# Residue-first keys and values for the strided heads, a new order of their value products, and a new plan

## The chip, the cores and the metric

The kernel runs on one core of one Trainium2 chip. The metric is the device time of one execution in microseconds (us); lower is better. A run gives the median of several executions, and one more execution is recorded by the hardware profiler.

## The reference

Inputs are q, k and v of shape 8 x 8 x 576 x 64 (batch, head, position, head width) and the weights of a mixture of four experts. First comes attention with two masks: heads 0 to 3 see the last 32 positions ("local"), heads 4 to 7 see every earlier position with the same position modulo 32 ("strided"):

```python
scores = scale * np.matmul(q, k.transpose(0, 1, 3, 2))
rel = pos[:, None] - pos[None, :]
mask_local = (rel >= 0) & (rel < 32)
mask_strided = (rel >= 0) & (pos[None, :] % 32 == pos[:, None] % 32)
attn = softmax(np.where(mask, scores, -1e9))     # mask by head
x = np.matmul(attn, v)                           # heads side by side: 8 x 576 x 512
```

Then, for each of the four experts, causal attention of width 64 over x (products with wq, wk, wv, all scores, softmax, product with wo); a gate picks two experts for each position and weights their outputs. The output is 8 x 576 x 512, float32.

## The kernel before, in words

**Stages.** Work is done by batch (8) and head pair (`hp`, 4 per batch: two local, two strided). `stage1(b, hp)` does the masked attention of one head pair; its result, transposed, goes as a high and a low part (`xh`, `xl`) into `project` (products with wq and wk), `values2` (product with wv, gate), `attend` (the experts' attention) and `out_tile` (product with wo, store).

**Strided stage 1.** There are 16 such stages (8 batches, 2 head pairs). Since position p sees only positions of its residue p mod 32, the work is cut by residue: 18 positions share one residue, and three residues at a time form a block of 54 queries against 54 keys, 11 blocks in all (the last has two residues). The steps:

- `load` (L454) brings q and k as 32 x 32 pieces into `nat`, eight DMAs of 32 partitions per head pair. `turn` (L465) transposes each of the two in one VectorE instruction (128 x 576) into `qkt`, where head width lies on partitions and positions along the row. For q the output is written residue first (a strided write, so that the 18 positions of a residue are neighbours); for k it is written in the order of positions.
- `scores` (L509) multiplies 64 x 64 quarters of TensorE's array: stationary is a run of 64 queries, moving are 54 keys. As k is in the order of positions, the moving operand is a pattern of 18 groups of 3 neighbours, 32 positions apart. A product of float32 is two instructions, so 24 products are 48 matmul records for each stage. The four quarters (row half by head, column half by block) are taken in turn.
- `mask`, `softmax` on VectorE, GpSimd and ScalarE; `tps2` (L568) transposes the probabilities; two copies bring them to `ptt`.
- `load_v` (L483) brings V by residue: 6 parts of 2 DMAs. Each DMA has the 18 positions of one residue of each of 5 or 6 blocks, and writes them to 18 partitions, every third one: within a block the key order is position first, residue second (`vt.t[64 * hb + r:64 * hb + r + 52:3, ...]`).
- `values1` (L619) multiplies V (stationary, 54 x 64) with the transposed probabilities (moving, 54 columns): 22 products, 44 matmul records. The row half of the array is the block's parity `hb`, the column half is the head `h`. The loops run over `i` (head and block, the head outermost), `hf`, `hb`: for one head's 11 products two quarters take turns, and then the other two.

**The order of the work.** Nothing in the program's loops sets the order: every operation is put down as an `Op` with an engine, and `PLAN`, a list of 2555 words, gives the order in which they are issued and, in the digits at a word's end, the buffer that each new tile takes (`223P564044` is operation 223 on TensorE with six new buffers). Some copies may stand on ScalarE or VectorE (letters A and D). Each engine works through its part of the list in that order; so does SyncE, from whose queue all DMAs are issued (634 of them). Buffers: `nat` 3, `qkt` 2, `v1` 3, PSUM banks 8.

Of the kernel before, what the change touches and what calls it, by code (L numbers as in the profile page):

```python
# [20 lines left out]
def attention_moe_kernel(  # L21
# [12 lines left out]
    nc = tc.nc  # L34
    B, H, S, D = q.shape
# [4 lines left out]
    STR = 32  # L40
    NJ = S // STR
# [49 lines left out]
    def op(kind, eng, n, key, fn, r=(), w=(), mode=None, npk=0, after=()):  # L91
# [24 lines left out]
        82S0 0P0 84S 4S1 40S2 41S 3S 39S 1S 42S 81S 52S0 2S 172S0 78S 80S 50S 5P120 160S1 8P34 6D 7A 43P561 11S1 10A  # L116
        46P70 9D 45A 44D 119S1 15P210 47A 48A 173A0 13S 174D0 53P431 117S 17D 161A0 16D 118S 162G0 19D0 121S 54D 21G
        55D 123S 23A 56D1 57D 77S 58G 18D 79S 59G 25D 60A 62D 122S 20G 61A 63D 129S2 22A 64D 83S 24D 66G 26D 12S 65G
        85D0 14S 27G 124S 28G 67D0 157S 120S 86D 169S 29D1 93P650 175S2 51S 126D1 30P701200 158A 163S3 95D 159G 49S
        94D 170A 91S1 97D2 37A 171G 33A 96D 35A 88S 31A 38D 176A 36D 98G 34D 87S 125D 164A 99G 100A 90S 68P435611  # L120
        177G 101A 92S 102D 165G 103D 133P211 89S 71A 32D 69A 104D 73A 75A 132S 70D 106G 1157P00 74D 134D 130S 1151P7
        105G 135D 1191P41 136D3 131S 1197P5 72D 138G 76D 107P211 184S0 137D 1192P 140A 139G 109D 108A 128S 142D 141A
        110P3622 205S2 143D 1163P1 187S1 113A 144D 115A 114D 1158P 111A 145G 116D 185A0 1169P2 178S 112D 146G 186D0
        1159P 127S 1164P 166S 147P630 202S 1170P 149A 148D 181S 188A 1193P 1198P 179A 189D 150P3633 180D 190S 1152P
        167A 271S0 155A 168D 1165P 153A 151A 156D 203S 1153P 154D 152D 1171P 182A 211S0 1199P 183D 1172P 199S 191A
        1160P 192D 1173A 204S 1166P 1161A 1174D0 1154P 234S1 1167A 1162D 1175G0 1178P60 1155A 1168D 235S 1156D 209S
        1221P320 200S 1179A 1216P010 1222D0 1247P760 245S1 1218D 1224A 1223D 201S 1226P310 1217D 1220A 1249D1 1219A
        1194P 210S 1225A 1228D 1176P2 206S 1195A 1227D 1230A 1248D 267S 1229A 1196D1 1182P0 237S 1177A 207D0 1251A
        232S 1231D 1250A 233S 1200P 208D 1184P6 212S 1183A 1201A 265S 1202D 302S2 213P131 1185A 236S 240D1 1203P7
        239S 215D 1180P4 238S 214D 216D1 276S2 1254P20 280S 1181A 217G 1204P 1186D00000 272S 1209P0 1205P 266S 218A  # L130
        269S 241D 1187A 301S 1188D 246P560 268S 242S 219D 1232G 1210P 193S0 1190G 1236G 247D 304S 1211P 248D 1233G
        220D 303S 1212P 1234G 273D0 1252P3 270S 1213A 221G 1238P141 1189S 1240A 307S 1214D 1239A 1237G 1253D 243S
        194A0 222D1 1215G1 244S 1255D 223P564044 279S 274D 195G0 1256A 338S1 249D0 1206P 341S 228A 1235G 224A
        281P130 229D 230A 226A 225D 314S0 1207A 250G 231D 1257D 300S 1208D 283D 1275P241 1258G 277S 251A 282D
        1241P500 1276D2 369S0 1280P731 1259G 284D2 1278A 1261P122 1242A 306S 1260G 1281D 1262A 1282D 1243A 312S
        1285P571 1277D 1283A 285G 252D 1264P133 337S 1284A 1267P04 1287D 372S 1279A 286A 1286D 1311P71 311S 253D
        1289A 1244P500 287D 305S 254G 1288A 1312D3 278S 1268A 288D 1265A 335S 1290D 289G 1245A 255D0 1266A 336S
# [12 lines left out]
        1369D00001 1374P5 1384A 1385D1 1370A 1371D 1386G1 1423P30 1375A 359P724122 1424D 1404G 1376D 1407G  # L150
        392P063533 446S2 366A 1405G 364A 367D 360A 365D 362A 1403G 416S 361D 363D 417P140 1373G 399A 1406G 397A 451S
        400D 393A 398D 395A 1408G 394D 452P721 540S1 396D 419D 504S 418D 1409P530 453D 584S0 1329P011 1411A 420D2
        1410A 511S 454D 421G 539S 455D3 1377P6 1332A 1330A 477S 1333D 422A 456G 512D1 448S 423D 538S 1425P4 1378A
        1380P1 457A 475S 1426D 424D 1427A 541S 1379D 425G 458D 471S 1340P70 1381A 1428D 414S 459D 1430G 513D 1372S
        1337P31 447S 1341A 460G 1331D 480D0 544S 474S 1429G 1412P521 1382D 1338A 426P461 449S 1413D 1414A 1431G
        1432P072 428A 1451P131 427D 450S 1434A 1435P253 1433D 1446P641 610S0 1453D0 1436A 461P700 1437A 1452D
        1438P23 1455A 463D 1456P511 1440A 462D 1439A 1415P022 1448D 1454A 1457D 1450A 1458D 1459A 1447D 1441P3 479D
        1416A 1460A 1417D 573S2 1449A 429P7200 1444A 575S 1442A 1461D 1445D 464P4511 1464G 1443D 432A 542S 434A 433D
        430A 1465G 518P161 435D 543S 467A 469A 431D 1463G 465A 468D 578S 470D 1462G 485P030 466D 1466G 579S 519D
        520D 1467G 585S 1468P270 487D 1477P541 537S 486D 1469A 1470A 521D1 1471P161 572S 1526P30 1473A 1479D1 574S  # L160
        522G 1472A 1478D 587S 1481A 488D0 515S1 523A 1537P00 545D1 1527A 576S 489G 1480A 582S 1482P21 1538A 1528D0
# [9 lines left out]
        1499A 1342S 598D 1620P121 599A 1586P041 640S 556D3 1585A 1625P761 1584A 643S 1511P31 1621D4 1588A 557G 1626D
        1623A 684S 1627D 1587A 1622D 1629A 641S 1597P50 1624A 1512D 675S 1508P12 558A 1598D 549S 1628A 559D 1513S
        1599P4 1509A 678S 560D 1551P7 1600D 561G 547S 648D1 1601A 1546S 644S 1500P6 1602D 1552A 1603G 551S 1553D
        673S 1604G 1589P211 1503A 1501A 583S 1504D 1605G 1502D 550S 649D 1606P032 1590A 709S 1630P511 1608A 1607D
# [830 lines left out]
```

## Time and profile before

| what | value |
|---|---|
| median of 3 runs | 544.49 us (540.88 to 545.86) |
| the profiled execution's own time | 546.64 us |
| its span, first to last instruction | 544.9 us |
| mean granted TensorE clock | 0.899 of full |
| TensorE matmul busy | 461.7 us, 85% |
| VectorE, ScalarE, GpSimd busy | 359.3, 259.9, 199.8 us |

The profiled execution is one execution: its rows give durations and waits, and its own time is 2.15 us above the median of the runs. "Busy" for TensorE is pipelined, so that 85% doesn't say that the array is at its peak.

### The profile page before, as it was taken

The page shows a single profiled execution, that of the slowest core. Times are in us where ns is not written, and L with a number is a line of the kernel's source. Part 1 is how long each engine was busy: PE and PEld are TensorE (multiplying, and loading weights), DVE is VectorE, ACT ScalarE, POOL GpSimd, SP SyncE. Part 2 cuts the span into 40 slices and gives each one's busy share as a digit, 9 for nine tenths or more (in the row PEclk, how much of TensorE's full clock was granted, in tenths as well). Part 3 has the DMA queues.
Part 4 walks back from the last instruction along what each step waited for, and adds up shares of the span by engine and source line. Part 5 has one row for each costly group of instructions (what it writes and reads, how often), then busy time and mean ns, then how long its engine had stood idle before and what let it go on. Part 6 is the DMA issues. An engine that isn't in the chain of part 4 may idle for free.

```text
span 544.9 us, 18754 instructions
## 1 busy us (share of the span) xinstructions
PE 461.7 (85%) x7594; PEld 410.3 (75%) x7594; DVE 359.3 (66%) x1090; ACT 259.9 (48%) x775; POOL 199.8 (37%) x318
## 2 busy tenths in 40 slices
PE   4456986579998998789897997799988898799996
PEld 3355975459887997588876996689767887689875
DVE  3861679367777887479687685678866666543670
ACT  2231627243545566355454374546464354543672
POOL 5450047325343444243162534161550514240260
PEclk8568888589989999799999999899889979879999
DMA  9623644445434453235245503354542401300112
GB/s 142 108 61 74 115 86 82 92 82 111 76 66 70 80 107 92 60 81 104 43 105 117 89 13 67 79 105 76 111 84 43 97 1 37 116 2 2 36 63 97
DMA packets 204215, 41.88 MB, mean 77 GB/s; under 512 B 199265, under 2 KB 199265, under 8 KB 204129
## 3 DMA queue, kind: packets, MB, share of 16 engines
q1 hardware_dynamic: 204128, 40.68, 37.4%
q8 instruction: 60, 0.98, 0.8%
q14 instruction: 27, 0.21, 0.1%
HBM read 31.20 MB, written 9.44 MB: 75 GB/s over the span
## 4 chain that ended last, share of the span: by engine, by line
PE 50%; SPq 23%; DVE 10%; DMA 7%; issue 6%; ACT 1%; POOL 1%; POOLq 0%; DVEq 0%; ACTq 0%
SPq L483 11%; PE bank L726 10%; PE bank L673 7%; PE bank L898 6%; SPq L454 6%; PE bank L927 6%; PE bank L811 5%; SPq L476 4%; PE bank L619 4%; PE bank L865 4%; DMA nat<-in_k_dram 3%; PE bank L504 2%; PE bank L597 2%; DVE qkt L465 2%; DMA nat<-in_q_dram 2%
## 5 line engine op out<-in xcount | busy, mean ns | idle before, releaser
L846 POOL TENSOR_SCALAR p<-p,st,wt 128x128 f32<-128x128 f32 (+3 forms) x128 | 76.5, 613 | 121.1 <-DVE st L830 48.9
L465 DVE STREAM_TRANSPOSE qkt<-nat 128x576 f32<-128x576 f32 x60 | 53.7, 898 | 49.4 <-DMA nat<-in_k_dram 25.9
L823 ACT ACTIVATE p<-p,st 128x512 f32<-128x512 f32 (+3 forms) x128 | 71.4, 563 | 6.3 <-DVE st L818 6.2
L294 ACT COPY th<-bank 128x384 f32<-128x384 f32 (+2 forms) x115 | 45.3, 433 | 46.6 <-PE bank L865 45.0
L818 DVE CUSTOM_DVE_ANT_0 p<-bank,m_cau 128x384 f32<-128x384 f32 (+3 forms) x128 | 56.9, 484 | 7.4 <-PE bank L811 6.9
L865 PE MATMUL bank<-ident,p 64*128 64x64 f32 x800 | 44.4, 239 | 12.9 <-DVE th L294 6.2
L898 PE MATMUL bank<-th,vs 128*64 128x192 f32 (+4 forms) x512 | 53.4, 360 | 0.3 <-issue 0.3
L865 PEld LDWEIGHTS bank<-ident,p 64*128 64x128 f32 x800 | 37.2, 149 | 21.3 <-POOL p L840 4.2
L898 PEld LDWEIGHTS bank<-th,vs 128*64 128x64 f32 x512 | 36.3, 147 | 17.1 <-issue 8.6
L746 ACT CAST qk<-bank 128x288 fp32r<-128x288 f32 x64 | 25.4, 397 | 45.0 <-PE bank L726 39.1
L582 DVE TENSOR_TENSOR xl<-bank,xh 128x128 fp32r<-128x128 f32 (+3 forms) x112 | 30.9, 325 | 23.5 <-ACT xh L580 23.2
L673 PE MATMUL bank<-wh_v,xh 128*128 128x260 f32 (+1 forms) x160 | 46.3, 289 | 0.0
L673 PE MATMUL bank<-wl_v,xh 128*128 128x260 f32 (+1 forms) x160 | 45.7, 285 | 0.0
L673 PE MATMUL bank<-wh_v,xl 128*128 128x260 f32 (+1 forms) x160 | 45.5, 284 | 0.0
L580 ACT CAST xh<-bank 128x128 fp32r<-128x128 f32 (+3 forms) x112 | 27.3, 324 | 29.5 <-PE bank L619 19.6
L748 DVE TENSOR_TENSOR qkl<-bank,qk 128x288 fp32r<-128x288 f32 x64 | 28.2, 444 | 15.1 <-ACT qk L746 14.9
L538 POOL TENSOR_TENSOR p1l<-p1l,st 128x640 f32<-128x640 f32 (+1 forms) x18 | 20.5, 1142 | 45.6 <-DVE st L536 43.0
L509 PE MATMUL bank<-qkt 64*64 64x54 f32 x768 | 19.2, 263 | 18.1 <-DVE qkt L465 14.2
L726 PE MATMUL bank<-xh,wh_q 128*128 128x288 f32 x112 | 34.3, 306 | 0.0
L726 PE MATMUL bank<-xl,wh_q 128*128 128x288 f32 x112 | 33.9, 303 | 0.0
L726 PE MATMUL bank<-xh,wl_q 128*128 128x288 f32 x112 | 33.7, 301 | 0.0
L726 PE MATMUL bank<-xh,wh_k 128*128 128x288 f32 x112 | 33.2, 296 | 0.0
(146 smaller groups left out, 1275.2 us busy)
## 6 DMA issues: line engine op xcount, KB each, us to landing
nat<-in_k_dram SPq DMA_DIRECT2D x120, 72.0 KB
nat<-in_q_dram SPq DMA_DIRECT2D x120, 72.0 KB
out_dram<-ys SPq DMA_DIRECT2D x32, 256.0 KB
v<-in_v_dram SPq DMA_DIRECT2D x96, 40.0 KB
v<-in_v_dram SPq DMA_DIRECT2D x128, 22.5 KB
v<-in_v_dram SPq DMA_DIRECT2D x64, 27.0 KB
v<-in_v_dram SPq DMA_DIRECT2D x32, 48.0 KB
out_dram<-ys SPq DMA_DIRECT2D x8, 128.0 KB
```

The source lines that it names most:

```text
L294: (nc.scalar.copy if e == "ACT" else nc.vector.tensor_copy)(dst, src)
L454: nc.sync.dma_start(nat.t[r0:r0 + 32, x].rearrange("p (n i) -> p n i", i=32), bass.AP(tensor=base.tensor, offset=base.offset + 32 * c, ap= ...
L465: nc.vector.transpose(dst, src)
L483: nc.sync.dma_start(vt.t[64 * hb + r:64 * hb + r + 52:3, h, :nm, :], bass.AP(tensor=base.tensor, offset=base.offset + h * S * D + (3 * hb ...
L673: nc.tensor.matmul(vp.t[:m, :NV], xx.t[:, t0:t0 + m], ww.t[:, kt, :], start=i == 0, stop=i == 11)
L726: nc.tensor.matmul(pj.t[:, :HS], ww.t[:, kt, ep * 128:(ep + 1) * 128], xx.t[:, c], start=i == 0, stop=i == 11)
L818: lambda e, sp=sp, p=p, a=a, nk=nk, ci=ci: nc.vector.tensor_tensor_reduce(out=p.t[:, a, :nk], in0=sp[a].t[:, :nk], in1=m_cau[:, S - nk:], ...
L823: op("exp2", "A", nk, k_ + 1, lambda e, p=p, a=a, ci=ci, nk=nk: nc.scalar.activation(p.t[:, a, :nk], p.t[:, a, :nk], AF.Exp, bias=st.t[:, ...
L846: lambda e, p=p, a=a, ci=ci, t=t, nk=nk: nc.gpsimd.tensor_scalar(p.t[:, a, :nk], p.t[:, a, :nk], st.t[:, 14 + ci + a:15 + ci + a], wt.t[:, ...
L865: nc.tensor.transpose(tp[hf].t[:, 64 * c:64 * c + 64], src, ident[r, r])
L898: nc.tensor.matmul(acc.t[o, c0:c0 + cn], vw, th[a].t[:, s0:s0 + cn], start=j == 0, stop=j == idx[-1], skip_group_check=True)
L927: nc.tensor.matmul(yp.t[:, :DM], xx.t[:, c0:c0 + 128], ww.t[:, ep, :], start=i == 0, stop=i == 5)
```

## The change

Four things. The key's transpose of strided heads is now written residue first, like the query's. So the keys of a block are a plain run of 54 columns, and the score product's moving operand has no pattern. The order of keys within a block is then residue first, so the mask `m_str` is built for that order, and the V of one residue goes to 18 neighbouring partitions. The loops of `values1` take another quarter at each step. `PLAN` is a new list of the same 2555 operations; 106 copies and small differences that may stand on one of two engines change to the other; in sum ScalarE has two operations more and VectorE two fewer, and TensorE, GpSimd and SyncE have as many as before. The row of zeros behind `qkt` grows from 8 to 18 columns.

```diff
     PLAN = """
-        82S0 0P0 84S 4S1 40S2 41S 3S 39S 1S 42S 81S 52S0 2S 172S0 78S 80S 50S 5P120 160S1 8P34 6D 7A 43P561 11S1 10A
...
     for hf in range(2):
-        v_ = m_str[64 * hf:64 * hf + 64].rearrange("p (u r) -> p u r", r=3)
-        keep(v_, [[-1, NJ], [-NJ, 3]], 0, 1)
-        keep(v_, [[0, NJ], [NJ, 3]], NJ - 1, -1)
+        v_ = m_str[64 * hf:64 * hf + 64].rearrange("p (r u) -> p r u", u=NJ)
+        keep(v_, [[-NJ, 3], [-1, NJ]], 0, 1)
+        keep(v_, [[NJ, 3], [0, NJ]], NJ - 1, -1)
...
-    QKT = fixed("qkt", [128, 2 * S + 8], 2, value=lambda t: [t[:, 2 * S:]])
+    QKT = fixed("qkt", [128, 2 * S + 18], 2, value=lambda t: [t[:, 2 * S:]])
...
             def turn(e, x):
                 src, dst = nat.t[:, x], qkt.t[:, x * S:x * S + S]
-                if x == 0 and not local:
+                if not local:
                     src = src.rearrange("p (u j) -> p u j", u=NJ)
                     dst = dst.rearrange("p (j u) -> p u j", u=NJ)
                 nc.vector.transpose(dst, src)
...
                 for h in range(2):
-                    nc.sync.dma_start(vt.t[64 * hb + r:64 * hb + r + 52:3, h, :nm, :],
+                    nc.sync.dma_start(vt.t[64 * hb + 18 * r:64 * hb + 18 * r + 18, h, :nm, :],
...
                             nc.tensor.matmul(sp[h].t[64 * c:64 * c + 64, 54 * i:54 * i + 54],
                                              qkt.t[r0:r0 + 64, 54 * g:54 * g + 64],
-                                             at(qkt.t, r0, 64, S + 3 * g, [[STR, NJ], [1, 3]]), start=True, stop=True)
+                                             qkt.t[r0:r0 + 64, S + 54 * g:S + 54 * g + 54], start=True, stop=True)
...
             def values1(e):
-                for i in range(6):
+                for m in range(3):
                     for hf in range(2):
-                        for hb in range(2):
-                            h, m = divmod(i, 3)
+                        for h, hb in ((0, 0), (1, 1), (1, 0), (0, 1)):
+                            i = 3 * h + m
                             g, mm = 2 * m + hb + 6 * hf, m + 3 * hf
```

## Rows read from the trace of the kernel before

**Rows 1.** The page's span and part 1, busy time of each engine.

```profile
span 544.9 us, 18754 instructions
PE 461.7 (85%) x7594; PEld 410.3 (75%) x7594; DVE 359.3 (66%) x1090; ACT 259.9 (48%) x775; POOL 199.8 (37%) x318
```

**Rows 2.** The page's part 4, the chain that ended last, by engine and line.

```profile
PE 50%; SPq 23%; DVE 10%; DMA 7%; issue 6%; ACT 1%; POOL 1%; POOLq 0%; DVEq 0%; ACTq 0%
SPq L483 11%; PE bank L726 10%; PE bank L673 7%; PE bank L898 6%; SPq L454 6%; PE bank L927 6%; PE bank L811 5%; SPq L476 4%; PE bank L619 4%; PE bank L865 4%; DMA nat<-in_k_dram 3%; PE bank L504 2%; PE bank L597 2%; DVE qkt L465 2%; DMA nat<-in_q_dram 2%
```

**Rows 3.** Stretches of 25 us: engines' busy us (instructions), granted clock, DMA share, GB/s.

```profile
0.00:25.00 25.00, 10.04 (x210) 8.33 (x210) 14.79 (x42) 6.86 (x16) 13.48 (x32) 0.67 0.81 122
25.00:50.00 25.00, 17.12 (x371) 15.43 (x371) 12.81 (x34) 6.82 (x22) 8.50 (x12) 0.72 0.31 66
50.00:75.00 25.00, 21.56 (x256) 20.53 (x256) 14.56 (x43) 11.94 (x36) 2.19 (x5) 0.86 0.57 106
75.00:100.00 25.00, 15.74 (x406) 13.29 (x406) 18.26 (x57) 13.07 (x41) 17.34 (x26) 0.81 0.44 82
100.00:125.00 25.00, 18.73 (x386) 15.46 (x387) 16.85 (x41) 8.78 (x22) 5.47 (x5) 0.72 0.51 92
```

**Rows 4.** PE timeline, value products (L619): start, us, matmul records, idle before.

```profile
52.86 2.36 PE L619 MATMUL bank<-pt,v 54*64 54x54 f32 x44 [4.94 <-ACT wh_q L384]
...
105.44 2.39 PE L619 MATMUL bank<-pt,v 54*64 54x54 f32 x44
...
168.67 2.42 PE L619 MATMUL bank<-pt,v 54*64 54x54 f32 x88
...
476.28 4.19 PE L619 MATMUL bank<-pt,v 54*64 54x54 f32 x88
```

**Rows 5.** Timeline around 103 and 456 us: strided score products (L509).

```profile
103.13 1.55 PE L509 MATMUL bank<-qkt 64*64 64x54 f32 x48 [6.04 <-DVE qkt L465]
...
456.38 1.69 PE L509 MATMUL bank<-qkt 64*64 64x54 f32 x96
```

**Rows 6.** Stretches that hold those groups alone; the clock is the third figure from the end.

```profile
103.00:107.80 4.80, 4.67 (x105) 4.38 (x105) 3.23 (x9) 0.86 (x2) 1.08 (x1) 0.50 0.59 103
168.60:171.10 2.50, 2.50 (x102) 2.39 (x105) 1.28 (x7) 1.48 (x7) 1.57 (x4) 1.00 0.47 80
...
456.30:458.00 1.70, 1.70 (x108) 1.57 (x101) 1.17 (x5) 0.63 (x3) 0.00 (x0) 1.00 0.15 33
```

**Rows 7.** DVE timeline: a strided q turn, then a k turn; then the page's L465 group.

```profile
80.35 1.25 DVE L465 STREAM_TRANSPOSE qkt<-nat 128x576 f32<-128x576 f32 x1 [0.97 <-DMA nat<-in_q_dram]
...
84.20 0.78 DVE L465 STREAM_TRANSPOSE qkt<-nat 128x576 f32<-128x576 f32 x1 [0.76 <-DMA nat<-in_k_dram]
...
L465 DVE STREAM_TRANSPOSE qkt<-nat 128x576 f32<-128x576 f32 x60 | 53.7, 898 | 49.4 <-DMA nat<-in_k_dram 25.9
```

**Rows 8.** Who waits at L465 and L509: us in total, times, longest.

```profile
DVE qkt L465 <- DMA nat<-in_k_dram: 25.9, 14, 5.8
...
DVE qkt L465 <- DMA nat<-in_q_dram: 15.1, 11, 3.9
...
PE bank L509 <- DVE qkt L465: 14.2, 2, 8.2
```

**Rows 9.** DMA issues of V, strided (L483) and local (L476): ns min/median/max.

```profile
L483 SPq DMA_DIRECT2D v<-in_v_dram x192: 762/762/1089, 19.7 to 471.6; - x192
...
L476 SPq DMA_DIRECT2D v<-in_v_dram x128: 312/436/1845, 7.4 to 432.9; - x128
...
L454 SPq DMA_DIRECT2D nat<-in_k_dram x120: 311/487/1924, 0.8 to 433.4; - x120
```

**Rows 10.** SyncE's queue from 43 to 52 us: DMA issues.

```profile
43.31 1.57 SPq L483 DMA_DIRECT2D v<-in_v_dram  x2
...
45.98 2.06 SPq L483 DMA_DIRECT2D v<-in_v_dram  x2
...
50.23 1.61 SPq L483 DMA_DIRECT2D v<-in_v_dram  x2
```

More of the change, by code (lines that the diff above doesn't have):

```diff
@@ L121, in attention_moe_kernel @@
[L121 to L125, printed above, removed]
@@ L171, in attention_moe_kernel @@
[L171 to L174, printed above, removed]
-        1591D 1609P473 562P630 1611A 1631D 1612P02 1610A 1514P70 1632D 563A 1614A 1613D 1634A 564D 1633A 1505P51
@@ new lines, in attention_moe_kernel @@
+        94D 28G 123S 97D1 54D 52S 99G 96D 27G 56D2 101A 160S 55D 58G 175S 103D 29D0 51S 98G 60A 62D 100A 30P072100
+        121S 57D 163S3 102D 59G 161A 125D1 122S 37A 35A 162G 61A 88S 33A 176A 36D 104D 31A 177G 130S0 63D 32D 106G
+        164A 64D 166S 34D 126D 65G 128S 66G 89S 38D 133P341 165D 105G 67D1 127S 167A 134D 68P562011 168G 92S 135D
+        136D3 1163P70 137D 90S 138G 73A 71A 74D 1151P1 69A 72D 75A 139G 140A 1197P31 70D 131S 76D 1157P4 142D 141A
+        1158P 87S 143D 1169P2 144D 129S 1170P 145G 107P650 146G 234S0 109A 108D 132S 147P051 149A 148D 190S0
@@ new lines, in attention_moe_kernel @@
+        1315A 1291G 369S 1246D 1293G 277S 319D3 256P762155 1295G 1271A 1273A 1274D 374S 1272D 320G 343D0 1297P340
+        372S 263A 259A 264D 257A 368S 260D 1299A 258D 1294G 321A 1298D 275S 1300P501 344D 261A 290P160 370S 1302A
+        1306P741 322D 1301A 312S 292A 377D1 1303P311 291A 315S 323D 1307D 324G 279S 349P050 1304A 376D 1309A 310S
+        1305D 325P611 350D 382P731 378S1 262D 326A 1308D 327A 351D 403S0 293P0200 1310A 383D 437S2 352D0 328P6111
+        294A 471S1 296A 298A 295D 1337P42 407S 353G 333A 297D 299D 331A 440S 329A 332D 334D 477S 330D 354A 1334P50
@@ new lines, in attention_moe_kernel @@
+        1525D 1473A 482S1 526G 1491P572 649D 1472A 1561P240 1493A 1592P360 1568D3 484S 1492A 1562D 1570A 1563D
+        1494P753 1567D 1571P020 1564A 1342S 1594D 1565A 610S 588P410 1496A 1593D 540S 1596A 1573D 1474P600 1336S
+        1595A 589D 674S0 590D 1575A 676S 1572D 1535P5 1569A 586S 591D1 1574A 545D1 516S 592G 1475A 1537P3 1495A
+        1536A 1576D 1476D 593A 527D1 1551P21 1538A 594D 546D 1533P4 1552A 1553D1 713S2 595D 1511P12 481S 1534A 596G
+        1543D00000 609S 1554P0 1512A 585S 1544A 483S 1545D 1599P7 1555A 1548P5 680S 1600D 1577G 1556D 1581G 613S
@@ new lines, in attention_moe_kernel @@
+        1559D 616D 1560G1 551S 1606P452 1515A 562P010 1608D 547S 1607A 1609P763 563D 564A 1630P321 1610A 1611D 778S1
+        1612P54 1631D 1505P10 1614A 1632D 1633A 1613D 1634A 600P0700 1506A 1635D 1637G 1507S 565P6311 605A 1639G
+        650S 601A 606D 654P421 603A 1636G 570A 602D 568A 1640G 571D 566A 652S 604D 621P510 567D 1638G 656D 677S
+        1641G 655D 1642P730 711S 623D 1651P021 622D 673S 1643A 1644A 569D 624D2 777S 1645P411 1656P51 708S 1646A
+        1652D5 625G 1508P72 1647A 756S2 1657D 1654A 1653D 618S0 626A 681D0 1658P6 1509A 1694P30 653S 1655A 627D 620S
@@ new lines, in attention_moe_kernel @@
+        1669A 1671P53 1743D 780S 1746A 1796P610 1765D1 754S 1673A 1737P271 1672A 1797D3 1791P341 1767A 1764D 689P560
+        1516S 782S 1799A 1793D 1798D 724P041 1766A 783S 1739D 691D 720S0 1712P1 1800A 725D 1795A 1792D 846S 690D
+        1794A 726D 748S 1741A 1679P70 1738D 1713A 749S 727D1 1740A 747S 1745A 785D0 728G 851S 1706P6 1680A 722S
+        1747D 692D3 729A 723S 1708P0 693G 1707D 730D 684S 752D1 694A 1728P3 746S 1709D 845S 695D 849S 731D 1710P5
+        1729A 1681S 696D 732G 1730D 688S 1722P4 1711A 743S 697G 1714D00001 721S 1731G1 1685P22 685S 1723A 1724D
@@ new lines, in attention_moe_kernel @@
+        1715A 753S 1716D 1770P10 1686A 1768P7 847S 1748G 1517P61 1769D 776S 1751G 1771D 745S 1752G 1772A 719S
+        1615P022 1750G 1518D 1749G 1773D 1718G 1774G 784D 1674P333 1616A 1618A 1775G 1617D 814S1 1619D 751D 1753G
+        813S 1754P542 1675A 1717S 1677A 1676D 733P270 1678D 1755A 1756D 1757P163 718S 734A 735D 698P031 1759A
+        1777P540 1758D 700A 1801P271 815S 1778A 1779D 699A 917S0 1780P611 1776G 1803D 1822P351 1781A 919S 1802D
+        1782A 1805A 816S 1783P40 1823D2 736P7600 1804A 1824D 1825A 701P1211 1806D 819S0 1785D 1807G 739A 1760P322
@@ new lines, in attention_moe_kernel @@
+        1826A 740D 1808G 1784D 786S1 1809G 702A 704A 703D 706A 1812G 1687S 737A 1786P5 705D 707D 1761A 787S 1810G
+        738D 741A 1762D 1811G 812S 742D 790P040 1787A 1789A 755S 1788D 1790D 757P121 791D 792D 1813P732 852D0
+        1874P60 1815A 1814A 759D 758D 793D2 1886P50 1875A 760D0 794G 1876D0 1829P01 853D 1887A 761G 1688P40 795A
+        796D 882S2 1877G0 762A 1868P3 789S 1689D 763D 913S 797D 1884P7 788S 1869A 764D 798G 1870D 818D1 916S 1827P2
+        1519S 765G 1885A 1880P1 822S 1828D 799D0 811S 1830D 1878P6 810S 1881A 766D1 1831A 809S 821S 1832D 1871P5
@@ new lines, in attention_moe_kernel @@
+        1879A 1834G 1833G 1882P4 1835G 1872A 817D 1873D 1865P3 945S1 1883A 1888D00000 885S 881S 1682P72 918S 1866A
+        886S 1867D 1889A 1890D 952S 1816P203 1683A 914S 1906P160 1892G 1817D 1818A 823S 1836P540 1911P371 1907D4
+        1837A 1908D 1909A 1839P021 1838D 884S 1937P150 1913D 1910A 1690S 1912D 1840A 1842P64 1915A 1841D 880S
+        1916P700 1938D5 1844A 912S 1914A 1819P300 1843D 1940A 1917D 1918D 1919A 1845P2 1939D 1920A 1820A 1921D 1941A
+        1927G 1821D 860P411 1848A 1924G 1846A 1849D 1847D 825P670 1925G 861D 862D 1926G 800P053244 826D 1922G 827D
@@ new lines, in attention_moe_kernel @@
+        871D 1952A 870A 1954P471 1953D 859S 1975P251 1972D0 1956A 1955A 1971D 1957P01 1974A 1976D 947S 1965P671
+        1958A 1934P411 1959D 1978A 1967D 1966D 1977D 1969A 1968A 1960P300 1979A 1935A 1973A 1936D 872P2000 1963A
+        1961A 1980D 1964D 1985G 1962D 837P1711 891S1 877A 875A 1981G 878D 873A 926P650 840A 1984G 876D 842A 874D
+        950S 838A 841D 1986G 843D 982S 893P431 839D 1983G 949S 927D 1982G 928D 1852S 1987P022 894D 1996P711 1989A
+        895D 1988A 953D0 2003P61 2045P50 1998D1 896D2 2000A 2049P41 954D 2046A 897G 2047D0 2001P2 1054S1 2050A 1997D
@@ new lines, in attention_moe_kernel @@
+        2048G0 2036P3 898A 892S 2002D 1999A 899D 922S 2039P0 2004D 2037A 900D 2005A 889S 2038D 901G 929D0 890S
+        2042P1 2040A 2006D 930G 902D1 956S0 2041D 2053P5 2007G 2043A 983S 931A 2044D 958S 2009G 932D 1859P42 2054A
+        1022S 2008G 933D 1052S 934G 924S 2113P70 1860A 1990P263 2114D3 1017S 2082P301 1991A 935D0 2010P150 987S
+        1992A 2077P470 2012A 2084D2 986S 2013P261 2011A 2079D 2087P500 2086A 1050S 2078D 2015D 2081A 980S 2016P17
+        2083D 2080A 2108P460 2088D 981S 2017A 2018D 2090A 1015S 2070P31 2110D 985S 2014A 2109D 2112A 1018S 2089D
@@ new lines, in attention_moe_kernel @@
+        2230A 2233D00000 2241P4 2239A 2240D 2234A 2235D 2346P61 2242A 1039P257044 2272G 2347D2 2243D 2268G
+        1072P136455 2269G 1130S1 1046A 1044A 1047D 2270G 1040A 1045D 1042A 1041D 1132P071 1131S 2267G 1043D 1079A
+        1073A 1080D 2293G 1075A 1074D 1077A 1076D 1097P250 1093S 1134D 2237G 2271G 1133D 2190P4 1126S 1098D 2294G
+        1135D1 1091S 1099D 1136G 2131P1 2191A 1078D 2193A 2236S 2192D 1100D3 1127S 1137A 2194D 2273P370 1101G 2134A
+        2132A 1138D 2341P021 1128S 2274A 2275A 2135D 2295G 2320P561 2133D 1102A 1129S 2342D 2207P41 2321D3 2344A
@@ new lines, in attention_moe_kernel @@
+        1096S 2343D 2323A 1103D 2201P30 2345A 1139D 2208A 2322D 1140G 2204P72 1104D 2324A 2202D 1105G 2203S 2276P101
+        2205A 1141P521 2277D 2278A 2296P462 1143A 1106P370 1142D 2298A 2299P013 2297D 1107A 2315P250 1108D 2301A
+        2302P64 2300A 2316D 2310P311 2303A 2317D 1109P7000 2318A 2304D 2312D 2319A 1144P2611 2311D 2314A 2279P511
+        1114A 1145A 1115D 1149A 1146D 1112A 2313A 1150D 1110A 2305P422 1113D 2325D 2280A 1111D 2328G 1147A 2281D
+        2330G 1148D 2348P1 2308A 2326G 2306A 2309D 2381P30 2307D 2331G 2349D 2350A 2327G 2329G 2351D 2390P0 2382A
@@ new lines, in attention_moe_kernel @@
+        2441G 2420D 2442G 2409P1 2373A 2440G 2443G 2374S 2206S 2438G 2364P333 2407S 2410A 2465G 2411D 2209S 2464G
+        2444P740 2439G 2365A 2367A 2366D 2486P060 2421G1 2368D 2446A 2445D 2447P521 2487D0 2491P131 2449A 2488D
+        2408G 2489A 2466G 2467P472 2448D 2512P021 2469A 2492D 2468A 2493D 2490A 2470P653 2481P711 2513D1 2494A
+        2450P422 2482D 2495A 2514D 2484A 2472D 2515A 2473P30 2483D 2471D 2369P70 2474A 2475D 2451A 2485A 2452D 2516A
+        2496D 2517P21 2370D 2502G 2378P52 2518D 2501G 2497G 2519P1 2379A 2498G 2375P61 2520D 2499G 2521A 2500G
@@ L263, in attention_moe_kernel @@
+        2503P300 2522D 2376A 2523G 2506P471 2505D 2504A 2377S 2476P2 2380S 2507A 2508D 2524G 2371S 2525G 2509P500
+        2479A 2477A 2480D 2478D 2526P162 2510A 2529P303 2528A 2527D 2511D 2532P47 2530A 2531A 2540P21 2534D 2533A
+        2543P62 2541A 2542S 2535P1 2544A 2545S 2546P30 2538A 2536A 2539D 2537D 2549P51 2547A 2548S 2552P02 2550A
+        2551S 2553A 2554S
     """
@@ L467, in stage1 @@
             for x in range(2):
-                op("turn" if x or local else "turn_s", "D", S, k0 - 13 + x, lambda e, x=x: turn(e, x), r=[nat[x]], w=[qkt[x]])
+                op("turn" if local else "turn_s", "D", S, k0 - 13 + x, lambda e, x=x: turn(e, x), r=[nat[x]], w=[qkt[x]])
         def load_v(e, i):
```

214 lines of the change are left out of this document (78 added, 136 removed).

## The prediction

> **What bounds the kernel now.** I read the page's busy line first: TensorE is busy 461.7 us of a span of 544.9 [rows 1], so 83 us of it are gaps; every other engine is below 70%. Then the chain: 50% of the span ends on TensorE, but 23% on SyncE's queue, from which all DMAs are issued, 11% (60 us) on L483 alone, the strided V loads; the value products L619 have 4% and the transposes L465 2% [rows 2]. So there are two near bounds, TensorE's work and the pace at which loads are issued. Then the stretches: in the first 125 us TensorE is busy 10.0 + 17.1 + 21.6 + 15.7 + 18.7 = 83.2 us, which leaves 41.8 us of gaps there, and the granted clock is 0.67 to 0.86 [rows 3], a mixture of the two levels; after 125 us the other 41 us of gaps lie over 420 us. Last the lines that the change touches: the two kinds of product, their clock, the turns and their waits, the V issues [rows 4 to 10].
>
> **Value products.** A stage has 44 matmul records, and there are 16 stages. At full clock two stages (88 records) take 2.42 us [rows 4], the clock 1.00 there [rows 6]. Taking about 0.22 us off for the last record's own run, the records begin every 2.20 / 87 = 25.3 ns. The nearest row for what the change makes of them is the strided score product: also 64 x 64 quarters and 54 columns, also row halves in turn, but all four quarters in turn. There 96 records take 1.69 us at full clock [rows 5, 6]: (1.69 - 0.22) / 95 = 15.5 ns. At half clock 44 value records take 2.39 us and 48 score records 1.55 us [rows 4 to 6]; with 0.31 us taken off, 48.4 and 26.4 ns. If values take the pace of scores, a stage saves 44 x 9.8 ns = 0.43 us at full and 44 x 22 ns = 0.97 us at half clock. Four stages now run at half clock (the groups at 52.9 and 105.4 us, and the pair at 476.3, whose 4.19 us for 88 show it [rows 4]); twelve at full. Sum: 12 x 0.43 + 4 x 0.97 = 9.0 us. Bounds: nothing at one end (two quarters of unlike rows already overlap, and a third may add nothing); at the other each quarter keeps the pace that two in turn show, 2 x 25.3 = 50.6 ns for one, so 12.7 ns with four: 12 x 0.55 + 4 x 1.06 = 10.8 us. A loss is excluded by the scores' row, which change rows and columns alike. On the path: the sixteen stages take some 12 x 1.21 + 4 x 2.2 = 23.3 us, and the chain gives L619 4% of 544.9 = 21.8 [rows 2]. I take 8 us.
>
> [...]
>
> **Score products.** Their moving operand becomes a plain run. The trace has no such product with four quarters and a plain run. Bounds: 15.5 ns as now, and 12.7 ns as above (26.4 and 24.2 at half clock): 48 records x 2.8 ns = 0.13 us in twelve stages, 48 x 2.2 = 0.11 in four, 2.0 us in all. A loss is excluded, since nothing is added. I take 1 us.
>
> **Key turns.** A strided q turn takes 1.25 us, a k turn 0.78 [rows 7]; the output pattern is the difference, and k gets it. 16 x 0.47 = 7.5 us more on VectorE (359.3 to 367, 67%). Most lies beside other work: VectorE is idle 49.4 us just before the 60 turns, waiting for loads [rows 7], and what it holds back is softmax steps of other stages. On the path: the chain has 2% or 11 us of the turns' 53.7, one fifth, and keys land later than queries (25.9 us of waits against 15.1 [rows 8]), so the k turn stands before the scores more often than the q turn. I take a third, 2.5 us; bounds 0 and 7.5.
>
> **V loads.** The issue of one strided V DMA takes 762 ns, smallest and median alike, of a local one 436 [rows 9]. The change leaves 192 issues of the same number of partitions and runs; only the step between partitions falls from three to one. Bounds: as now, or down to 436 ns, 192 x 0.326 = 63 us off SyncE's queue, of which 11% of 544.9 x 0.326 / 0.762 = 26 us stands on the chain. A dearer issue I exclude, since the pattern gets simpler. The row that stays nearest is the same instruction's own, 0 us, but two things differ between the two lines, the step and the count of 18 against 32, and no row parts them. So the lower end is a rival.
>
> [...]
>
> **The plan.** It moves operations by several places on every queue. I added up SyncE's issues in both lists, at 0.49 us for a q or k piece, 0.44 and 0.76 for V [rows 9] and about 0.04 between issues. Up to the last V of batch 0 there are 44.8 us of issues instead of 46.3; in the old run that V is the issue at 50.2 [rows 10], and TensorE's wait of 4.94 us ends at 52.9 [rows 4]. In batch 1 the fourth pair's q and k come 9 us earlier (78.8 against 87.7), the third pair's V 8 us later (100.4 against 92.0), the fourth's V stays (102.0, 103.0). The value products of these two pairs stand side by side in the new list, so the last V of batch 1 releases both, about when it did. Nearly the same issue time has to pass, so I take 0. Bounds: each long wait in the start can go or come again, 4.94 and 6.04 us [rows 4, 5], so 11 us off or 6 us on. Where the new list makes V late, the value product waits at the head of TensorE's queue with the projections behind it. Mask, zeros and the copies' engines: 0; two operations less on VectorE make up 1 us of the 7.5.
>
> **Sum.** 546.6 (the profiled execution) - 8 - 1 + 2.5 + 0 = 540.1 us, 1.2% less. That execution is 2.15 us above the median of the runs, 544.5; the same step from the median gives 538. A measurement of this kernel tells about 1% from no change: below 539.0 or above 549.9.
>
> **Rivals.**
> 1. *Loads set the pace.* For it: 23% of the chain on SyncE's queue, and the 42 us of gaps in the first 125. Against: L619 itself is on the chain for nearly all its time. Then half of the products' gain turns into waits for V, and two thirds of the k turns show: 546.6 - 4.5 + 5 = 547, from the median 545. No change.
> 2. *The k turn stands before the scores* (slower). Both masks and the whole softmax of a stage wait for it, and VectorE works strictly in order. The place is the wait of L509 for L465, 14.2 us now in two waits [rows 8], the longest followed by work at a clock of 0.50 [rows 6]. Price: all 7.5 us on the path, and the products' gain lost in the gap that they then meet, 554 from the profile, 552 from the median. It decides from the point where more than about three quarters of the turns are on the chain; they are one fifth now.
> 3. *The V issue falls to 436 ns.* For it: it's the only line with a step of three, and the costliest load to issue. Against: 5 or 6 runs cost the same 762 ns, so the price hangs on something that needn't be the step. Price: half of the 26 us on the chain, the rest taken by TensorE as the bound: 540.1 - 13 = 527, from the median 525.
> 4. *The columns add nothing*, so that the change doesn't do what it says: values stay at 25.3 ns, and 546.6 - 1 + 2.5 = 548, from the median 546.
>
> **Chances.** Forecast 0.46, its own range 530 to 545, so 0.39 faster and 0.07 the same; first rival 0.18, the same; second 0.17, slower; third 0.11, faster; fourth 0.08, the same but for 0.01 slower. Faster 0.50, same 0.32, slower 0.18. The range is cut inside the third rival and at the second's time: 524 to 552.
>
> **What would show it.** Right: L619 at 88 records in 1.4 to 1.6 us at full clock; L509 at 96 in 1.4 to 1.7; 32 strided turns of 1.25 us; L483 still at 762 ns; TensorE busy about 452 us; the gaps in the first 125 us near 42. Wrong: L483 near 440 ns (third rival), L619 still at 2.4 us (fourth), more waits of L509 for L465 than 14 us (second), TensorE's busy time down by 9 us and the gaps up by as much (first). A start whose long waits are gone would make the time fall below the forecast without any of the four edits.

## The result, and the profile after

The changed kernel takes 478.12 us in the median (475.73 to 482.8, 4 runs), the kernel before 545.17 beside it: a ratio of 0.8792, 95% interval 0.8707 to 0.8877. That is 67 us or 12% less. The forecast was 538, the range 524 to 552: the direction was right and the size wrong by a factor of ten (6.5 us forecast).

The profiled execution after, the span and part 1 of its page, and the two lines of its chain (part 4), which answer to [rows 1, 2]:

```profile
span 477.3 us, 18746 instructions
PE 424.9 (89%) x7594; PEld 380.4 (80%) x7594; DVE 363.3 (76%) x1088; ACT 258.4 (54%) x777; POOL 199.2 (42%) x318
...
PE 75%; DVE 7%; SPq 4%; issue 4%; DMA 4%; POOL 2%; ACT 2%; POOLq 0%; DVEq 0%; ACTq 0%
PE bank L726 16%; PE bank L673 11%; PE bank L898 9%; PE bank L927 8%; PE bank L811 7%; PE bank L865 6%; PE bank L504 3%; PE bank L597 3%; PE bank L509 3%; PE bank L619 3%; PE bank L737 3%; PE bank L791 2%; SPq L476 2%; DMA nat<-in_q_dram 2%; DMA nat<-in_k_dram 2%
```

Three things stand there. SyncE's queue fell from 23% of the chain to 4%, and L483, which had led the list with 11%, isn't among the fifteen lines named. TensorE's gaps fell from 83 to 52 us. And TensorE's busy time fell by 36.8 us, four times what the products alone were to save; the same 7594 matmuls ran, and the granted clock of the whole run rose from 0.899 to 0.953. Two wide stretches show it, up to 125 us and from there on (the row of before, then of after; the clock is the third figure from the end). First before:

```profile
0.00:125.00 125.00, 83.19 (x1629) 73.05 (x1630) 77.28 (x215) 47.46 (x137) 46.98 (x80) 0.75 0.53 93
125.00:544.00 419.00, 378.53 (x5967) 337.25 (x5965) 282.04 (x876) 212.43 (x638) 152.77 (x239) 0.94 0.34 72
```

And after:

```profile
0.00:125.00 125.00, 91.52 (x1832) 82.13 (x1837) 92.73 (x260) 57.02 (x169) 52.78 (x89) 0.85 0.60 109
125.00:477.00 352.00, 333.37 (x5790) 298.24 (x5772) 270.58 (x828) 201.42 (x609) 146.40 (x229) 0.99 0.37 80
```

In the first 125 us 1832 matmul records are done instead of 1629, at a mean clock of 0.85 instead of 0.75. The loss of before wasn't in the start alone: behind it the gaps were 419 - 378.5 = 40.5 us, and are now 18.6, at a clock of 0.99 instead of 0.94.

The lines that the change touches, after. V's issues (ns min/median/max, [rows 9]), then SyncE's queue at 34 us, where 16 of them follow each other:

```profile
L483 SPq DMA_DIRECT2D v<-in_v_dram x192: 273/334/1397, 11.5 to 405.0; - x192
...
33.72 7.34 SPq L483 DMA_DIRECT2D v<-in_v_dram  x16
```

The median fell from 762 to 334 ns, below the 436 ns of the local V that I had taken as the lowest possible. By these medians 192 x 0.428 = 82 us have left SyncE's queue. (Some issues last longer than the median: the 16 in a row take 7.34 us, 0.46 apiece with the space between them.)

Value products, score products, turns, in their timelines (start, us; [rows 4, 5, 7]), and the clock of the first two stretches:

```profile
305.65 1.60 PE L619 MATMUL bank<-pt,v 54*64 54x54 f32 x88
...
226.24 1.62 PE L509 MATMUL bank<-qkt 64*64 64x54 f32 x96
...
74.15 1.26 DVE L465 STREAM_TRANSPOSE qkt<-nat 128x576 f32<-128x576 f32 x1 [0.64 <-DMA nat<-in_q_dram]
76.34 1.25 DVE L465 STREAM_TRANSPOSE qkt<-nat 128x576 f32<-128x576 f32 x1
...
L465 DVE STREAM_TRANSPOSE qkt<-nat 128x576 f32<-128x576 f32 x60 | 61.2, 1024 | 10.6 <-DMA nat<-in_k_dram 7.2
...
305.60:307.30 1.70, 1.70 (x108) 1.61 (x110) 1.29 (x6) 1.35 (x7) 0.77 (x2) 1.00 0.00 0
226.20:227.80 1.60, 1.60 (x99) 1.50 (x97) 1.60 (x9) 1.60 (x6) 0.00 (x0) 1.00 0.21 45
```

88 value records take 1.60 us instead of 2.42; 96 score records 1.62 instead of 1.69; all turns together 61.2 us instead of 53.7, the 7.5 us that the forecast had. But the idle time before the turns went from 49.4 to 10.6 us: loads that VectorE waited for are now there.

### The profile page after: what moved, and what is told of

The parts are those of the page before. It is cut to its first block, busy times and chain, and to the rows that moved or that the text cites. A ratio compares the mean times of both kernels' runs of the same rounds, so it can differ in the third digit from the quotient of the medians.

```text
span 477.3 us, 18746 instructions
## 1 busy us (share of the span) xinstructions
PE 424.9 (89%) x7594; PEld 380.4 (80%) x7594; DVE 363.3 (76%) x1088; ACT 258.4 (54%) x777; POOL 199.2 (42%) x318
## 3 DMA queue, kind: packets, MB, share of 16 engines
q1 hardware_dynamic: 204128, 40.68, 42.1%
## 4 chain that ended last, share of the span: by engine, by line
PE 75%; DVE 7%; SPq 4%; issue 4%; DMA 4%; POOL 2%; ACT 2%; POOLq 0%; DVEq 0%; ACTq 0%
PE bank L726 16%; PE bank L673 11%; PE bank L898 9%; PE bank L927 8%; PE bank L811 7%; PE bank L865 6%; PE bank L504 3%; PE bank L597 3%; PE bank L509 3%; PE bank L619 3%; PE bank L737 3%; PE bank L791 2%; SPq L476 2%; DMA nat<-in_q_dram 2%; DMA nat<-in_k_dram 2%
## 5 line engine op out<-in xcount | busy, mean ns | idle before, releaser
L823 ACT ACTIVATE p<-p,st 128x256 f32<-128x256 f32 (+3 forms) x128 | 71.1, 560 | 6.5 <-DVE st L818 6.3
L465 DVE STREAM_TRANSPOSE qkt<-nat 128x576 f32<-128x576 f32 x60 | 61.2, 1024 | 10.6 <-DMA nat<-in_k_dram 7.2
L818 DVE CUSTOM_DVE_ANT_0 p<-bank,m_cau 128x256 f32<-128x256 f32 (+3 forms) x128 | 56.5, 483 | 3.8 <-PE bank L811 3.4
L294 ACT COPY th<-bank 128x384 f32<-128x384 f32 (+2 forms) x111 | 43.1, 432 | 23.8 <-PE bank L865 22.8
L898 PE MATMUL bank<-th,vs 128*64 128x192 f32 (+4 forms) x512 | 48.9, 340 | 0.3 <-issue 0.3
L898 PEld LDWEIGHTS bank<-th,vs 128*64 128x64 f32 x512 | 34.1, 138 | 14.0 <-issue 7.2
L865 PE MATMUL bank<-ident,p 64*128 64x64 f32 x800 | 41.2, 231 | 3.5 <-POOL p L846 3.5
L865 PEld LDWEIGHTS bank<-ident,p 64*128 64x128 f32 x800 | 35.0, 143 | 10.1 <-POOL p L846 4.2
L582 DVE TENSOR_TENSOR xl<-bank,xh 128x270 fp32r<-128x270 f32 (+3 forms) x112 | 30.9, 325 | 12.7 <-ACT xh L580 12.2
L538 POOL TENSOR_TENSOR p1s<-p1s,st 128x648 f32<-128x648 f32 (+1 forms) x18 | 20.8, 1158 | 37.8 <-DVE st L536 33.3
```

Of the source, the lines that this page charges most:

```text
L294: (nc.scalar.copy if e == "ACT" else nc.vector.tensor_copy)(dst, src)
L465: nc.vector.transpose(dst, src)
L538: nc.gpsimd.tensor_tensor(P, P, bc[0], ALU.subtract)
L818: lambda e, sp=sp, p=p, a=a, nk=nk, ci=ci: nc.vector.tensor_tensor_reduce(out=p.t[:, a, :nk], in0=sp[a].t[:, :nk], in1=m_cau[:, S - nk:], ...
L823: op("exp2", "A", nk, k_ + 1, lambda e, p=p, a=a, ci=ci, nk=nk: nc.scalar.activation(p.t[:, a, :nk], p.t[:, a, :nk], AF.Exp, bias=st.t[:, ...
L865: nc.tensor.transpose(tp[hf].t[:, 64 * c:64 * c + 64], src, ident[r, r])
```

## The experiments

The four parts can be put in and taken out one by one, since the list of operations and the code hardly touch each other. Two theories at first: the *load theory* (the cheaper V issue did it, through SyncE's queue) and the *plan theory* (the new list did it). Ratios are to the kernel before, run on the same chip.

**The list alone, and all but the list.** The first is the kernel before with the new `PLAN`, the second the changed kernel with the old one:

```diff
     PLAN = """
-        82S0 0P0 84S 4S1 40S2 41S 3S 39S 1S 42S 81S 52S0 2S 172S0 78S 80S 50S 5P120 160S1 8P34 6D 7A 43P561 11S1 10A
...
```

> The kernel before with the new list of operations alone; V, keys and value products as before. Load theory (the cheaper V issue, 762 to 334 ns, is the main cause, since SyncE's queue paced the first half): the plan by itself gives little, 535 to 550 us, L483 still at 762 ns, TensorE busy near 460 us. Plan theory (the new order did most of the 67 us): 490 to 505 us, gaps of TensorE down to about 50 us with L483 at 762 ns.

Measured: 533.11 us, ratio 0.978 (0.9733 to 0.9828). Slightly below the load theory's range, far above the plan theory's.

> The changed kernel with the old list of operations; all four edits of the code are in. Load theory: most of the gain stays, 485 to 505 us, and the time at half clock falls from 112 us to under 70. Plan theory: 530 to 540 us, since then the edits bring only the 8 to 11 us of the products.

Measured: 489.33 us, 0.8968 (0.892 to 0.9017), at a granted clock of 0.958. The load theory's number: the list is worth 2%, the edits of the code 10%.

**V alone, and all but V.** One edit, put into the kernel before, and taken out of the changed one:

```diff
-                    nc.sync.dma_start(vt.t[64 * hb + r:64 * hb + r + 52:3, h, :nm, :],
+                    nc.sync.dma_start(vt.t[64 * hb + 18 * r:64 * hb + 18 * r + 18, h, :nm, :],
```

> The kernel before with one edit: V goes to neighbouring partitions. Keys stay in the order of positions, so keys and V of the strided heads don't pair. Load theory: 495 to 515 us, L483 near 334 ns, TensorE's busy time down by 20 us or more although no product was changed, because the clock is granted more of the time. Product or plan theory: 535 to 545 us, the freed queue time turns into waits for buffers.

Measured: 490.86 us, 0.8989 (0.894 to 0.9039): this one line brings 54 of the 67 us, a little more than the load theory's range had. Part 1 and the chain of its page, and V's issues:

```profile
PE 443.3 (90%) x7594; PEld 395.3 (80%) x7594; DVE 361.0 (73%) x1090; ACT 258.8 (53%) x775; POOL 199.5 (41%) x318
...
PE 74%; DVE 8%; SPq 6%; issue 5%; DMA 3%; POOL 2%; ACT 2%; POOLq 0%; DVEq 0%; ACTq 0%
...
L483 SPq DMA_DIRECT2D v<-in_v_dram x192: 273/331/1632, 19.5 to 418.1; - x192
```

No product was touched, and still TensorE's busy time fell from 461.7 to 443.3 us. The expectation of 20 us or more was nearly met. So a dear issue costs twice here: TensorE waits for the loads, and what it did behind the long waits ran at the lower granted clock (in the kernel before 0.50 in the 2 us behind each of the waits of 8.17, 4.94 and 6.04 us that end at 25.19, 52.86 and 103.13; in the profiled execution with V alone the clock of the whole run was 0.935 instead of 0.899).

> The changed kernel with V on every third partition again; keys residue first, new value order, new list. Keys and V of the strided heads don't pair. Load theory: 530 to 545 us, L483 at 762 ns, the early gaps and the half clock are back. Plan theory: 490 to 500 us, only some 15 us lost.

Measured: 532.6 us, 0.9771 (0.9707 to 0.9834), and the list alone had 0.978. So with the dear V issue the new keys and the new value order together bring nothing that can be measured.

**Is it the queue's time, or the way in which V lands?** The new partitions change both. Here the bytes and partitions stay as in the changed kernel, and only the number of issues doubles:

```diff
-                    nc.sync.dma_start(vt.t[64 * hb + 18 * r:64 * hb + 18 * r + 18, h, :nm, :],
...
-                                              ap=[[STR * D, NJ], [6 * D, nm], [1, D]]))
+                    for m0, m1 in ((0, 3), (3, nm)):
+                        nc.sync.dma_start(vt.t[64 * hb + 18 * r:64 * hb + 18 * r + 18, h, m0:m1, :],
...
+                                                  ap=[[STR * D, NJ], [6 * D, m1 - m0], [1, D]]))
```

> The changed kernel with each strided V DMA cut in two (blocks 0 to 2, then the rest): the same bytes to the same neighbouring partitions, but 384 issues on SyncE's queue instead of 192. At some 0.33 us and a gap of 0.04 that is 142 us of queue time, near the 154 us of the 192 issues of 762 ns. Load theory (the time on SyncE's queue is what the step of three cost): 520 to 535 us, as the new list with V on every third partition, with half clock back in the first 250 us. Rival (what cost was the landing or the writing of V on every third partition, and the issue time only showed it): 475 to 485 us.

Measured: 522.67 us, 0.953 (0.9461 to 0.96). V's issues, and the chain of its page:

```profile
L484 SPq DMA_DIRECT2D v<-in_v_dram x384: 273/323/1784, 11.5 to 454.4; - x192
...
PE 61%; SPq 17%; DVE 7%; DMA 6%; issue 6%; ACT 2%; POOL 0%; DVEq 0%; ACTq 0%; POOLq 0%
```

SyncE's queue is back at 17% of the chain, with V's issues at 323 ns each. 384 x 0.323 - 192 x 0.334 = 60 us more queue time cost (0.953 - 0.8792) x 545 = 40 us. V lands here as in the changed kernel, so issue time alone, with no step of three, costs as much for each microsecond as V's did (0.67 here; 55 us for 83, or 0.66, with V alone). The pages bear on landing too (part 3, the DMA queue: packets, MB, share of the time of 16 engines; before, then after):

```profile
q1 hardware_dynamic: 204128, 40.68, 37.4%
q1 hardware_dynamic: 204128, 40.68, 42.1%
```

37.4% of 544.9 us is 203.8, 42.1% of 477.3 us is 200.9: the packets are as many and take nearly the same time with a step of three and with neighbours. So a step of three made the issue dear, and not the transfer.

**Is it the step or the count of 18?** Two of three residues of a block go to every second partition, one to neighbours:

```diff
-                    nc.sync.dma_start(vt.t[64 * hb + 18 * r:64 * hb + 18 * r + 18, h, :nm, :],
+                    p0 = 64 * hb + 17 + r
+                    if r == 0:
+                        nc.sync.dma_start(vt.t[64 * hb:64 * hb + 18, h, :nm, :], src_)
+                    else:
+                        nc.sync.dma_start(vt.t[p0:p0 + 35:2, h, :nm, :], src_)
```

> The changed kernel, where two of the three residues of a V block go to every second partition (18 partitions each, interleaved) and one to 18 neighbouring ones; keys and V of the strided heads don't pair. If any step but one makes an issue dear, 128 of the issues take 762 ns and 64 take 334, and the time is 505 to 520 us. If the price grows with the step or with the span of partitions, the 128 lie between, near 550 ns, and the time is 490 to 505 us. If only steps that aren't powers of two are dear, all 192 are near 334 ns and the time is that of the changed kernel, 476 to 484 us.

Measured: 511.27 us, 0.9353 (0.9274 to 0.9432; two executions). The two lines of issues in one and the same run, neighbours first:

```profile
L487 SPq DMA_DIRECT2D v<-in_v_dram x64: 273/337/1352, 32.2 to 440.8; - x64
L489 SPq DMA_DIRECT2D v<-in_v_dram x128: 762/779/1502, 11.6 to 442.0; - x128
```

18 partitions in both, in one execution, and 337 against 779 ns: a step of two costs what a step of three does, and the count of 18 isn't what made the issue dear. The time is the one expected if any step but one is dear.

**Where along the run?** A step of three in batches 4 to 7 alone:

```diff
+                    p0, st_ = (64 * hb + 18 * r, 1) if b < 4 else (64 * hb + r, 3)
+                    nc.sync.dma_start(vt.t[p0:p0 + 17 * st_ + 1:st_, h, :nm, :],
```

> The changed kernel with V on every third partition in batches 4 to 7 alone (96 issues of 762 ns; keys and V of the strided heads don't pair there). If SyncE's queue paces the kernel all through, half of the loss comes, 503 to 510 us; if it does so in the first half only, where the start has to catch up, 480 to 490 us.

Measured: 502.77 us, 0.9231 (0.9154 to 0.9308). So half of the dear issues, all of them in the later half, cost about half: SyncE's queue paced the kernel all through. My own picture, in which the first 125 us were its place, was too narrow.

**The products and the keys.** The list and V without the other two parts; all but the value order; all but the keys:

```diff
-                for m in range(3):
+                for i in range(6):
                     for hf in range(2):
-                        for h, hb in ((0, 0), (1, 1), (1, 0), (0, 1)):
-                            i = 3 * h + m
+                        for hb in range(2):
+                            h, m = divmod(i, 3)
```

```diff
-                if not local:
+                if x == 0 and not local:
...
-                                             qkt.t[r0:r0 + 64, S + 54 * g:S + 54 * g + 54], start=True, stop=True)
+                                             at(qkt.t, r0, 64, S + 3 * g, [[STR, NJ], [1, 3]]), start=True, stop=True)
```

> The kernel before with the new list and V on neighbouring partitions; keys in the order of positions and the old order of value products, so keys and V of the strided heads don't pair. Load theory: these two carry nearly all: 478 to 486 us. Product theory: once loads no longer pace it the products' 9 us show, so that without them it is 486 to 492 us.

Measured: 480.16 us, 0.8776 (0.873 to 0.8821).

> The changed kernel with the old order of value products (two quarters in turn). TensorE's busy time rises by 6 to 7 us, L619 back at 2.4 us for 88 records. If TensorE is the bound now (75% of the chain), the time rises by 4 to 7 us to 482 to 486 us; if waits still absorb it, it stays within 2 us of the changed kernel's 478 to 480 us.

Measured: 481.95 us, 0.8833 (0.8799 to 0.8868). Part 1 of its page, beside 424.9 after, and the value products' group (records, busy us, mean ns, idle before) in the kernel before, in this one and in the changed one:

```profile
PE 432.3 (90%) x7594; PEld 388.3 (81%) x7594; DVE 364.2 (76%) x1088; ACT 258.0 (54%) x777; POOL 198.5 (41%) x318
...
L619 PE MATMUL bank<-pt,v 54*64 54x54 f32 (+1 forms) x704 | 24.6, 244 | 9.9 <-ACT wh_q L384 4.9 <-DMA v<-in_v_dram 2.6 <-issue 2.3
L619 PE MATMUL bank<-pt,v 54*64 54x54 f32 (+1 forms) x704 | 20.0, 221 | 0.3 <-ACT pt L294 0.3
L619 PE MATMUL bank<-pt,v 54*64 54x54 f32 (+1 forms) x704 | 14.4, 221 | 0.3 <-ACT pt L294 0.3
```

> The changed kernel with keys in the order of positions (plain key turn of 0.78 us, patterned score products); V stays on neighbouring partitions, so keys and V of the strided heads don't pair. VectorE has 7.5 us less. If the dear key turn stands on the path the time falls by 2 to 5 us to 474 to 477 us; if it is hidden, and the score products' 1 to 2 us count, it stays the same or rises by up to 2 us.

Measured: 480.01 us, 0.8777 (0.8734 to 0.8821). Part 1 of its page:

```profile
PE 429.3 (90%) x7594; PEld 384.4 (80%) x7594; DVE 357.5 (75%) x1088; ACT 258.3 (54%) x777; POOL 199.2 (42%) x318
```

All three intervals lie within that of the whole change (0.8707 to 0.8877). The new value order takes 20.0 - 14.4 = 5.6 us off the value products themselves (TensorE's 7.4 us less holds other lines too); the keys give VectorE 5.8 us more (363.3 beside 357.5 without them). Put side by side, the runs bound what each is worth in time. With keys in the order of positions, the value order changes nothing: 0.8777 with it, 0.8776 without, so 0 us, give or take 3.4. With the old value order, residue-first keys cost 0.8833 - 0.8776, 3 us, give or take 3: at the edge of the noise. With both in, neither can be told from nothing. What remains of the ratio is V and the list, and their own ratios give it: 0.8989 x 0.978 = 0.879.

**Can more be taken off the queue?** Among the rest, SyncE's queue still holds 40 stores. They go to ScalarE's queue in the first kernel, and the loads of the weights as well in the second:

```diff
-                nc.sync.dma_start(out[b, t0:t0 + 128, :], ys.t)
+                nc.scalar.dma_start(out[b, t0:t0 + 128, :], ys.t)
...
-                dma = nc.scalar if e == "ACT" else nc.sync
+                dma = nc.scalar
```

> The changed kernel with the 40 stores of the output issued from ScalarE's queue instead of SyncE's (some 18 us of issue time moved, and waits for the copies that precede stores leave SyncE's queue). If what is left of the loads' pace still costs 0.6 us for each us of queue time: 466 to 474 us. If TensorE's work is the bound now (75% of the chain): 475 to 482 us.

Measured: 505.6 us, 0.9261 (0.9178 to 0.9343). Neither expectation: 26 us slower than the changed kernel.

> As the one with stores on ScalarE's queue, and the 18 loads of the weights from there too (some 9 us of issue time that stands in the first 55 us, where TensorE is idle 15 of the first 30 us). If the start is paced by SyncE's queue: 5 to 8 us below the kernel with the stores alone. If the start waits for landings and the softmax chain: the same within 3 us.

Measured: 513.22 us, 0.9398 (0.9293 to 0.9503), slower still. From the waits of the kernel with the stores alone: two of ScalarE's, two of SyncE's queue (us in total, times, longest):

```profile
ACT p L823 <- DMA v<-in_v_dram: 12.1, 1, 12.1
ACT p1s L540 <- DMA v<-in_v_dram: 5.7, 1, 5.7
...
SPq L483 <- PE bank L597: 36.4, 7, 17.1
SPq L476 <- PE bank L619: 20.8, 3, 12.1
```

ScalarE, which takes no V, stands still for V loads, 17.8 us in two waits; without the move the same two waits of SyncE's queue are shorter:

```profile
SPq L483 <- PE bank L597: 24.7, 8, 7.6
SPq L476 <- PE bank L619: 10.4, 2, 5.8
```

The timelines show what ScalarE stands behind in the longer of its two waits (ScalarE's part, then SyncE's queue):

```profile
243.80 0.34 ACTq L939 DMA_DIRECT2D out_dram<-ys  x1
244.18 0.51 ACT L823 ACTIVATE p<-p,st 128x256 f32<-128x256 f32 x1 [12.08 <-DMA v<-in_v_dram]
...
241.91 0.80 SPq L483 DMA_DIRECT2D v<-in_v_dram  x2
```

ScalarE was idle from 232.1 us (244.18 - 12.08) on, a wait that the profile puts down to a V load; two V loads were issued from 241.91 on, the store (L939) at 243.80, and ScalarE's work went on at 244.18, behind the store. The wait of 5.7 us is put down to a V load too. In the trace of the changed kernel, where all 634 DMAs are on SyncE's queue, they use eight semaphores, V loads and stores the same ones, and each of the 40 stores waits for the semaphore that tells of its own landing. That in the same way a store on ScalarE's queue waits for a V load of SyncE's queue, so that shared semaphores tie the two queues together, is my estimate from these rows. How the 26 us add up from such waits no run took apart.

## Why the prediction was wrong

**The step that failed** is "V loads", the term taken at 0 because "two things differ between the two lines, the step and the count of 18 against 32, and no row parts them". That was true of the rows, and the choice fell on the wrong one: the issue fell to 334 ns, and V alone brought 54 us where the sum had 0. The step sets the price: 18 partitions cost 334 ns with a step of one, 779 with two, 762 with three. The argument in the third rival, that 5 or 6 runs cost the same 762 ns, showed only that the price doesn't follow the bytes; it said nothing for the count.

**The second failure is the size.** Had the third rival been the forecast it would still have been 525, and V alone gives 491, the list with V 480. Its price was the chain's share of L483, 60 us, times 0.43 = 26 us, and half of that. Both cuts were wrong. The gain reached the rest of the queue too: with V alone, SyncE's share of the chain fell from 23% (125 us) to 6% (30 us), some 95 us, though L483 had only 60 of them. And the granted clock was higher where gaps had closed (0.899 before with 83 us of gaps, 0.953 after with 52), which the sum left out. Measured, per microsecond of queue time: V alone 55 us for 83, or 0.66; the list without and with V (772 and 332 ns an issue) 55 for 84, 0.65; twice the issues 40 for 60, 0.67; the step of two 31 for 57, 0.54; the late half 24 for 41, 0.58. Some 0.6 each time, within the 0.1 to 0.15 that the intervals leave open, against my 13 for 63, 0.2. The first rival ("Loads set the pace") had the bound right and drew the wrong end from it: it let the V issue stand and concluded that nothing would change.

**The plan** was taken at 0, bounds -11 and +6; alone it gave -12 us (0.978), just outside. The sum of issue times covered the first two batches, up to some 103 us of 545. What in the new list brings the 12 us is not shown.

**Value products**: right as a mechanism, 1.60 us for 88 records at full clock, forecast 1.4 to 1.6. In that pair they begin every (1.60 - 0.22) / 87 = 15.9 ns, where scores were the model with 15.5. All sixteen stages fell from 24.6 to 14.4 us, where the sum had 9.0 off; of these 10.2 us, 5.6 are the order (20.0 with the old one), and the other 4.6 came with the rest of the change. The fourth rival had the records stay at 25.3 ns. They didn't: with rows in turn at each step before and after, the new columns took the pace from 25.3 to 15.9 ns. Whether it is loads or products that overlap more, no row here shows. But the 8 us on the path were not there. With the dear V issue nothing of them shows (all but V against the list alone: 0.9771 and 0.978), and with the cheap one the order alone is worth 0 us, give or take 3.4 (0.8777 and 0.8776). "L619 itself is on the chain for nearly all its time" doesn't mean that shortening it shortens the run; what takes the gain up once the loads come in time is not shown.

**Score products** 1.62 for 96 records instead of 1.69: 0.04 us a stage, under a third of the largest estimate. **Key turns**: the turns took exactly the 7.5 us more. In time, the 2.5 us forecast are neither shown nor excluded (3 us, give or take 3, with the old value order; 0.8792 with them against 0.8777 without, with the new one). The second rival, in which they decide, is excluded.

**What would show it**: L483 near 440 ns was listed as the sign of the third rival, and the profile after has it at 334. TensorE's busy time was to be 452 us, and 425 is the sign that the clock had moved, for which no line was given.

## What to carry to other kernels

When one queue issues all loads in order, add up its issue time by line and ask what each issue costs, not only what it moves; a microsecond of V's issues on that queue was worth some 0.6 us here, in the early half of the run and in the late one. Moving DMAs to another engine's queue is no sure way to get it (the 40 stores on ScalarE's queue made this kernel 26 us slower): look first at which semaphores the two queues share. Write a DMA's target on neighbouring partitions if the order of the data can be chosen to allow it (an issue of 0.33 us here instead of 0.76). And where TensorE's granted clock is lower behind a wait, as it was here (0.50 behind the one of 6.04 us), price the wait with the slow stretch that follows it.

## What the runs showed of the hardware that was not expected

- A DMA to 18 partitions, 5 or 6 runs of 256 bytes to each, takes its queue 0.33 us with neighbouring partitions and 0.76 to 0.78 us with every second or third one; a step of two cost what a step of three did. With 3 runs or fewer, to neighbours, it was 0.32 us.
- The dearer issue didn't make the transfer longer: the packets of the whole kernel took 203.8 us (over 16 engines) with a step of three and 200.9 with neighbours.
- An issue to 18 neighbouring partitions (334 ns) is cheaper than one to 32 with the same runs (436 ns for the local V before).
- With the stores on ScalarE's queue, ScalarE had two waits put down to V loads of SyncE's queue, of 12.1 and 5.7 us; the longer ended with a store's issue. The kernel with 40 stores there was 26 us slower, though some 17 us (40 x 0.42) had left SyncE's queue.
